# Gated linear attention feeding a GELU MLP: another row block releases W_in's first part, and two row transfers wait for a memset

## The chip, the cores and the metric

The kernel runs on one core of a Trainium2 chip. The metric is the device time of one execution in microseconds (us); lower is better. The engines are TensorE (PE; its weight loads are listed as PEld), VectorE (DVE), ScalarE (ACT), GpSimd (POOL) and SyncE (SP). SP and ACT issue transfers to a hardware queue of their own, POOL to a software queue. All three use the core's 16 DMA engines.

## The reference

Attention with a decaying state, in four batches of eight heads, 768 positions and 48 values a head; its output, as 3072 tokens of 384 values, goes through an MLP of width 2048.

```python
for t in range(S):
    state = alpha[:, :, t, :, None] * state + einsum('bhd,bhe->bhde', k[:, :, t], v[:, :, t])
    y[:, :, t] = einsum('bhd,bhde->bhe', q[:, :, t], state)
x = y.transpose(0, 2, 1, 3).reshape(B * S, H * D)
h = x @ w_in                                                     # 384 x 2048
g = 0.5 * h * (1 + tanh(sqrt(2 / pi) * (h + 0.044715 * h**3)))
out = g @ w_out                                                  # 2048 x 384
```

## The kernel before

**Tiling.** Positions are cut into six chunks of 128. A unit is one batch in one chunk; two units are a pair, and there are twelve pairs. For a pair, ACT takes the logarithm of alpha (`la`, L359), PE forms running sums over the 128 positions with a triangular matrix (`cum`, L346), and ACT takes exponentials of them with both signs (`b`, `binv`, L407). DVE scales q and k with these (`qp`, `kp`, L418). PE transposes the scaled rows (`qkT_ps`, L428) and multiplies them (`at`, L489), DVE masks the product (`atm`, L496), and PE makes `yps` from it and v (L546). It is narrowed (`x`), transposed (`xT`), and goes through the two MLP layers: `hT` (PE, L572, with W_in), GELU (ACT, L578), `acc` (PE, L591, with W_out). W_in lies in four tiles of 512 columns each, called parts 0 to 3 here; W_out in four as well.

**The order.** Every engine works through one list in order. For the first two pairs and some of the work behind them the order is written out by hand in `FIRST`: each step is an engine's letter and a task, as `P:cum0.0` (PE, first unit of pair 0) or `G:load.13` (POOL). The rest is placed by a planner with costs. The step `P:fill.7` puts seven products of a zero tile (`idle`, L289) on PE before the first `cum`.

**The loads.** Loads 0 to 11 are the row blocks of pairs 0 and 1, one unit of alpha, q or k each (192 KB). In order they are alpha of pair 0's two units (0, 1), q and k of its first unit (2, 3), q and k of its second (4, 5), alpha of pair 1's two units (6, 7), q and k of pair 1's first unit (8, 9), and q and k of its second (10, 11). SP issues all of them except 2 and 3, which ACT issues (`BY_ACT`). All other loads come from POOL, in the order of `LOADS`:

```python
LOADS = ('gatea 0 1', 'v0', 'gatek 0 1', 'in 0', 'v1', 'in 1', 'in 2', 'in 3', 'out 0', 'out 1', '2a', ...)
```

`v0` is v of pair 0, `in 0` is part 0 of W_in, `2a` the first unit's rows of pair 2. A `gate` step holds POOL: it is a copy of one column of a row block into a scratch tile (L314). It waits for that block's landing, and all of POOL's later issues stand behind it. `gatea 0 1` waits for load 1, and `gatek 0 1` for load 5 (k of pair 0's second unit). POOL has at most eight transfers outstanding. The ninth waits for the first to land, and so on.

PE reaches the first `hT` products in the order l10.0, l10.1, l10.3, l10.2, l10.5, l10.4, l10.6, l10.7 (`FIRST`); l10.n takes part n // 2 of W_in.

Of the kernel before, what the change touches and what calls it, by code (L numbers as in the profile page):

```python
# [7 lines left out]
F32 = mybir.dt.float32  # L8
# [163 lines left out]
class _Kernel:  # L172
# [3 lines left out]

    SPLIT = (2,)
    EARLY = (0, 1)
    LOADS = ('gatea 0 1', 'v0', 'gatek 0 1', 'in 0', 'v1', 'in 1', 'in 2', 'in 3', 'out 0', 'out 1', '2a', 'out 2', '2b', 'out 3', '3', '4', '5', '6', '7', '8', '9', '10', '11')

    PACKED, CUM_FF, R = (0, 1), (0, 1), 4
    RINGS = (('a', 0, 0, 1), ('a', 0, 1, 2), ('q', 0, 0, 1), ('k', 0, 0, 1), ('q', 0, 1, 2), ('k', 0, 1, 2),
# [436 lines left out]
    def tasks(self):  # L619
# [30 lines left out]
        for r, m, lo, hi in self.RINGS:  # L650
            loads[r, m, lo] = loads[r, m, hi - 1] = s.add(
                "load", {"ACT" if n in self.BY_ACT else "SP": W["ring_issue"]}, n, self.load(r, *pairs[m], lo, hi), land=(W["ring_v" if r == "v" else "ring"] * (hi - lo) // 2 if n else W["begin"]))
            n += 1
        for step in self.LOADS:
            if step[0] == "v":
# [209 lines left out]
    def run(self):  # L865
        nc, C = self.nc, self.C
        self.tasks()
        nc.vector.memset(self.zero, 0.0)
        nc.vector.memset(self.ones, 1.0)
        make_upper_triangular(nc, self.ut_h, val=1.0, diag=True)  # L870
        make_identity(nc, self.ident)
        nc.vector.memset(self.half, 0.0)
        for o in range(2):
            nc.vector.memset(self.half[64 * o:64 * o + 64, o:o + 1], 1.0)
        nc.vector.tensor_reduce(self.blk, self.ident.rearrange("p (g j) -> p j g", j=4), axis=mybir.AxisListType.X, op=ALU.max)
        same = self.blk[:, None, :].to_broadcast([C, C // 4, 4])
        nc.vector.tensor_tensor(self.ut_blk[1].rearrange("p (g j) -> p g j", j=4), self.ut_h.rearrange("p (g j) -> p g j", j=4), same, op=ALU.mult)
        nc.vector.tensor_tensor(self.ut_blk[0], self.ut_blk[1], self.ident, op=ALU.subtract)
        for i in range(max(self.BUFS[n] for n in self.ring)):
            for n in self.ring:  # L880
                if i < self.BUFS[n]:
                    nc.vector.memset(self.ring[n][i][:, :, :, self.D:64], 0.0)
        nc.vector.tensor_copy(self.ut, self.ut_h)
        order = self.s.order()
        for t in order:
            if t.load == LN_EXP:
                self.act_set(LN_EXP)
            t.emit(t.engine)
# [30 lines left out]
```

## Time and profile before

| | |
|---|---|
| median of 11 runs | 177.02 us |
| the runs, sorted | 176.65, 176.81, 176.89, 176.91, 176.93, 177.02, 177.61, 177.75, 177.83, 177.93, 178.12 |
| the profiled execution: its time | 178.63 us |
| the profiled execution: its span | 176.8 us |
| PE busy, of the span | 171.6 us (97%) |
| ACT busy | 128.8 us (73%) |
| DVE busy | 96.3 us (54%) |
| POOL busy | 57.7 us (33%) |
| moved by DMA | 28.86 MB, 163 GB/s |

The span runs from the first to the last instruction of the program; 1.83 us of the profiled execution lie outside of it. All times in the profile count from the start of the span. The chain of work that ended last is followed back from the last instruction, at each step to what released it. In the timeline a row merges like instructions that follow each other without a gap. A transfer's row gives its issue; its landing is a time from that issue on.

### The profile page before, as it was taken

To read this page: it belongs to the slowest core of one execution; us is meant where nothing else is said; L and a number is where in the kernel's file an instruction comes from. 1 tells how busy PE (TensorE), PEld (TensorE's weight loads), DVE (VectorE), ACT (ScalarE), POOL (GpSimd) and SP (SyncE) were. 2 spreads that over 40 slices of the span, in tenths; PEclk is the share of its full clock that TensorE was granted. 3 is DMA by queue.
4 is the path that set the end of the run, shared out by engine and by line. 5 is a ranking of instruction groups with operands and counts; after the bars stand their busy time and mean duration, and the time that the engine had idled before them with its cause. 6 is when DMAs were issued, how large, how long until landed. Compare 5 with 4: busy or idle time off the path is not lost.

```text
span 176.8 us, 4439 instructions
## 1 busy us (share of the span) xinstructions
PE 171.6 (97%) x1845; PEld 135.9 (77%) x1845; DVE 96.3 (54%) x191; ACT 128.8 (73%) x213; POOL 57.7 (33%) x64
## 2 busy tenths in 40 slices
PE   7899999999999999999999999999999999999993
PEld 2556899666886897797699689688697697796973
DVE  6289940066878996596499797494436415000000
ACT  2559799856977767858788967987988984481841
POOL 2596345996646766666530000000000000000000
PEclk9999999999999999999999999999999999999999
DMA  4999999999999999999999992262261360301102
GB/s 127 290 265 239 210 244 234 212 207 209 218 316 211 229 263 225 209 228 204 196 250 235 170 154 75 48 159 74 46 166 47 86 166 4 98 35 44 48 0 89
DMA packets 49621, 28.86 MB, mean 163 GB/s; under 512 B 37697, under 2 KB 46017, under 8 KB 49601
## 3 DMA queue, kind: packets, MB, share of 16 engines
q0 software_dynamic: 26464, 17.70, 60.3%
q1 hardware_dynamic: 22592, 10.49, 23.2%
q10 hardware_dynamic: 544, 0.39, 0.8%
q8 instruction: 14, 0.23, 0.6%
q14 instruction: 7, 0.05, 0.1%
HBM read 25.17 MB, written 4.72 MB: 169 GB/s over the span
## 4 chain that ended last, share of the span: by engine, by line
PE 93%; ACT 2%; DMA 2%; issue 0%
PE hT L572 36%; PE acc L591 35%; PE qkT_ps L428 4%; PE at L489 4%; PE yps L546 3%; DMA a<-in_alpha_dram 2%; PE yps L543 2%; PE kv L506 2%; PE cum L378 2%; PE cum L346 2%; PE idle L289 1%; PE xT_ps L560 1%; PE cum L380 1%; ACT qkT L446 1%; PE k_ps L454 1%; ACT la L359 1%
## 5 line engine op out<-in xcount | busy, mean ns | idle before, releaser
L572 PE MATMUL hT<-xT,w_in 128*128 128x256 bf16 x576 | 69.4, 273 | 0.0
L578 ACT ACTIVATE gT<-hT 128x512 bf16<-128x512 f32 x96 | 56.3, 600 | 17.7 <-PE hT L572 14.2
L591 PE MATMUL acc<-w_out,gT 128*128 128x384 bf16 (+3 forms) x416 | 69.0, 313 | 0.0
L572 PEld LDWEIGHTS <-w_in 128*128 128x128 bf16 x576 | 61.1, 113 | 1.6
L591 PEld LDWEIGHTS <-gT 128*128 128x128 bf16 x416 | 36.9, 97 | 19.2
L496 DVE TENSOR_TENSOR atm<-at,ut 128x512 bf16<-128x512 f32 x48 | 30.1, 682 | 12.7 <-PE at L489 12.6
L418 DVE TENSOR_TENSOR qp<-q,b 128x768 bf16<-128x768 f32 (+1 forms) x15 | 11.9, 795 | 14.9 <-ACT b L407 14.8
L418 DVE TENSOR_TENSOR kp<-k,binv 128x768 bf16<-128x768 f32 (+1 forms) x15 | 11.9, 792 | 10.6 <-ACT binv L407 10.6
L603 ACT COPY ot<-acc 128x384 f32<-128x384 f32 (+3 forms) x17 | 7.4, 439 | 13.0 <-PE acc L591 12.9
L308 POOL DMA_DIRECT2D q<-in_q_dram x11 | 12.2, 1105 | 7.5 <-DVE qp L418 1.8
L308 POOL DMA_DIRECT2D a<-in_alpha_dram x11 | 12.3, 1115 | 6.0 <-issue 2.2
L308 POOL DMA_DIRECT2D k<-in_k_dram x11 | 12.2, 1105 | 6.1 <-DVE st L531 2.4
L308 POOL DMA_DIRECT2D vb<-in_v_dram x11 | 12.1, 1101 | 4.8 <-DMA a<-in_alpha_dram 1.8
L407 ACT ACTIVATE b<-cum 128x768 bf16<-128x768 f32 (+1 forms) x15 | 10.3, 685 | 3.8 <-PE cum L380 2.3
L280 ACT ACT_TABLE_LOAD x9 | 11.5, 1283 | 0.9 <-PEq L903 0.7
L578 ACT ACT_TABLE_LOAD x9 | 11.5, 1283 | 0.2
L407 ACT ACTIVATE binv<-cum 128x768 bf16<-128x768 f32 (+1 forms) x15 | 10.2, 682 | 0.4 <-PE cum L350 0.4
L528 DVE TENSOR_TENSOR stmp<-kv,st 128x384 f32<-128x384 f32 x16 | 8.8, 553 | 2.0 <-PE kv L506 2.0
L446 ACT COPY qkT<-qkT_ps 128x512 bf16<-128x512 bf16 (+1 forms) x9 | 6.5, 728 | 4.2 <-PE qkT_ps L428 4.1
L553 DVE CAST x<-yps 128x384 bf16<-128x384 f32 x12 | 6.7, 556 | 5.0 <-PE yps L546 4.9
L531 DVE TENSOR_TENSOR st<-stmp,ends 128x384 bf16<-128x384 f32 x16 | 8.9, 558 | 0.6
L546 PE MATMUL yps<-vb,atm 128*128 128x48 bf16 x192 | 8.7, 183 | 0.1
(64 smaller groups left out, 158.1 us busy)
## 6 DMA issues: line engine op xcount, KB each, us to landing
out_dram<-ot SPq DMA_DIRECT2D x19, 192.0 KB, 5.2
a<-in_alpha_dram POOLq DMA_DIRECT2D x9, 384.0 KB, 11.9
q<-in_q_dram POOLq DMA_DIRECT2D x9, 384.0 KB, 11.5
k<-in_k_dram POOLq DMA_DIRECT2D x9, 384.0 KB, 11.4
vb<-in_v_dram POOLq DMA_DIRECT2D x9, 192.0 KB, 11.5
w_in<-in_moe_w_in_dram POOLq DMA_DIRECT2D x4, 384.0 KB, 8.9
w_out<-in_moe_w_out_dram POOLq DMA_DIRECT2D x4, 384.0 KB, 11.6
out_dram<-ot SPq DMA_DIRECT2D x9, 96.0 KB, 1.8
```

The costliest lines, as they stand in the source:

```text
L280: nc.scalar.add_instruction(mybir.InstLoadActFuncSet(name=nc.get_next_instruction_name(), act_func_set_id=i, engine=mybir.EngineType.Activ ...
L308: dma(u[t][:, lo:hi].rearrange("t b h d -> t (b h) d"), src.rearrange("b h s d -> s (b h) d")[c * C:(c + 1) * C])
L407: self.nc.scalar.activation(u[n].rearrange("t i h d -> t i (h d)")[:, lo:hi], cum, AF.Exp, scale=1.0 if n == "b" else -1.0)
L418: self.nc.vector.tensor_tensor(out, rows, b, op=ALU.mult)
L446: self.copy(e)(t, ps)
L496: self.nc.vector.tensor_tensor(u["atm", i][:, o], u["at", i][o], self.ut[:, None, :].to_broadcast([self.C, self.H // 2, self.C]), op=ALU.mult)
L528: nc.vector.tensor_tensor(s, acc, old, op=ALU.add)
L531: nc.vector.tensor_tensor(new.rearrange("f p (o d) -> f (p o) d", o=2), acc.rearrange("f p (o d) -> f (p o) d", o=2), ends, op=ALU.mult)
L546: nc.tensor.matmul(y[:, h, :], u["atm", i][:, h % 2, h // 2, :], u["vb"][:, i, h, :], start=c == 0, stop=True, skip_group_check=True)
L572: self.nc.tensor.matmul(h[:, s], w_in[:, j, nt % 4 + s], self.xT[c % self.NX][:, j, lo:hi].rearrange("p g t -> p (g t)"), start=j == 0, st ...
L578: return lambda e: self.nc.scalar.activation(self.gT[c % self.NG][:, nt:nt + 2, lo * self.C:hi * self.C], f.pop(("h", c, lo, nt)), AF.Gelu ...
L591: self.nc.tensor.matmul(f["acc", c, b][:, lo:hi], self.gT[c % self.NG][:, nt, b * self.C:(b + 1) * self.C], self.w_out[:, nt, lo:hi], star ...
```

## The change

Two edits. In `LOADS` the gate ahead of W_in's part 0 waits for another row block: `gatek 1 0` is load 9, k of pair 1's first unit. (The short title of the change speaks of q; the code names k, and the built program's copy into the gate tile reads k.) Its place in POOL's order stays. And in `run` the tile that loads 2 and 4 fill, q of pair 0, is made early, and DVE writes zeros into one column of its first unit. Load 2 writes the same place, so that ACT's issue of it now waits for this memset; load 3 stands behind it in ACT's queue. In DVE's list the memset stands third, after those of `zero` and `ones`. No other instruction moves on any engine.

```diff
-    LOADS = ('gatea 0 1', 'v0', 'gatek 0 1', 'in 0', 'v1', 'in 1', 'in 2', 'in 3', 'out 0', 'out 1', '2a', ...)
+    LOADS = ('gatea 0 1', 'v0', 'gatek 1 0', 'in 0', 'v1', 'in 1', 'in 2', 'in 3', 'out 0', 'out 1', '2a', ...)
...
         nc.vector.memset(self.zero, 0.0)
         nc.vector.memset(self.ones, 1.0)
         make_upper_triangular(nc, self.ut_h, val=1.0, diag=True)
+        first = self.p[0, 0]["q"] = self.tile("q", [C, 2, self.H, self.D], F32)
+        nc.vector.memset(first[:, 0, 0, 0:1], 0.0)
         make_identity(nc, self.ident)
```

More of the change, by code (lines that the diff above doesn't have):

```diff
@@ L178 @@
     EARLY = (0, 1)
-    LOADS = ('gatea 0 1', 'v0', 'gatek 0 1', 'in 0', 'v1', 'in 1', 'in 2', 'in 3', 'out 0', 'out 1', '2a', 'out 2', '2b', 'out 3', '3', '4', '5', '6', '7', '8', '9', '10', '11')
+    LOADS = ('gatea 0 1', 'v0', 'gatek 1 0', 'in 0', 'v1', 'in 1', 'in 2', 'in 3', 'out 0', 'out 1', '2a', 'out 2', '2b', 'out 3', '3', '4', '5', '6', '7', '8', '9', '10', '11')
     PACKED, CUM_FF, R = (0, 1), (0, 1), 4
```

## The prediction

> **What bounds the kernel now.** The page comes first. PE is busy for 97% of the span, and the chain that ended last is PE's for 93%. So in most of the kernel whatever moves PE moves the end by the same time. The chain in order of time then shows the stretch in which that isn't so yet.
>
> ```profile
> PE 171.6 (97%) x1845; PEld 135.9 (77%) x1845; DVE 96.3 (54%) x191; ACT 128.8 (73%) x213; POOL 57.7 (33%) x64
> PE 93%; ACT 2%; DMA 2%; issue 0%
> 0.74 3.91 DMA a<-in_alpha_dram
> 4.67 0.53 ACT la L359
> 5.25 1.44 PE cum L346 x7
> ```
>
> The head hangs on one transfer: alpha of pair 0's first unit, issued at 0.74, landed at 4.65. ACT's logarithm follows, then the running sums. From there on the chain runs through engines, PE mostly, and no other load is on it. From 18.4 on it is nearly all PE. So two things can matter: when the first alpha block lands, and whether a POOL load becomes late for PE. The timelines of POOL and PE give the second.
>
> ```profile
> 7.68 0.25 POOL L314 COPY gate<-k 128x1 f32<-128x1 f32 x1 [0.61 <-DMA k<-in_k_dram]
> 8.15 0.74 POOL L321 DMA_DIRECT2D w_in<-in_moe_w_in_dram  x1 [0.21 <-issue]
> 8.88 1.18 POOL L308 DMA_DIRECT2D v<-in_v_dram  x1
> 10.06 2.25 POOL L321 DMA_DIRECT2D w_in<-in_moe_w_in_dram  x3
> 21.84 1.47 PE L572 MATMUL hT<-xT,w_in 128*128 128x256 bf16 x12
> 23.35 0.83 PE L572 MATMUL hT<-xT,w_in 128*128 128x256 bf16 x6
> 24.35 0.82 PE L572 MATMUL hT<-xT,w_in 128*128 128x256 bf16 x6
> ```
>
> Asked one by one, W_in's four parts land 7.0, 8.3, 9.4 and 10.6 us after their issues at 8.15, 10.06, 10.79 and 11.56: at 15.2, 18.4, 20.2 and 22.2. PE first takes them at 18.39, 21.01, 22.49 and 24.35. Each is 2.2 to 3.2 us early. Part 3 has the least room, 2.2 us, at l10.6.
>
> **The hold on ACT's transfers.** It adds one DVE memset of 128x1 (60 ns by its neighbour `ones`). It delays `half` and what follows by that much, but `blk` waits for POOL's `ident` until 1.81 anyway, so this costs nothing. ACT's two issues started at 0.77 and 1.50. They now start at about 1.2, when the third memset is done, and 1.95: 0.45 us later. Who pays: q and k of the first unit landed at 4.5 and 5.1 and are taken at 7.33 and 7.81, so nobody does. Who gains is read from the queues between 2.0 and 4.2 us, where q10 is ACT's and q1 SP's:
>
> ```profile
> q10 hardware_dynamic: 384, 0.28, 51.0%
> q1 hardware_dynamic: 271, 0.20, 28.6%
> ```
>
> ACT's queue moved more than SP's, although the first alpha block (0.20 MB) was all that the head waited for. With ACT's start 0.45 us later and its mean rate of 0.15 MB/us (0.28 MB in 1.9 us) kept, and with the 335 GB/s that the window from 3 to 4 us shows for both, alpha's block is through at T, where 0.20 + 0.15 x (T - 2.7) = 0.48 - 0.335 x (4.2 - T). So T is 3.87, and it lands 0.33 us earlier. The ends: 0, if the slow start of SP's queue (5 packets up to 2.7 us) is its own; 0.85, if ACT's data stayed wholly behind it. I take 0.33. The second alpha block gains less, but its logarithm has 0.5 us to spare before `cum` on PE. The chain after it is made of engines' own times, and the loads it uses (k of pair 0 at 7.6, v0 at 11.8 for 13.56) are early enough. So PE would reach W_in 0.33 us sooner, unless W_in is late.
>
> **The moved gate.** It waits for load 9 instead of load 5. Load 5 landed at 3.10 + 4.4 = 7.55, and W_in's part 0 was issued 0.60 later. Load 9 was issued at 5.74, so it landed at 10.1; part 0 is issued at 10.7, 2.55 us later. Behind the gate stand all of POOL's loads: v1, W_in's other parts, W_out, and rows from pair 2 on. SP and ACT pass no gate. What the delay is worth depends on what the DMA engines do meanwhile, told by POOL's queue q0 in three windows (8.7 to 9.0, 11.2 to 11.5, 11.5 to 12.0):
>
> ```profile
> q0 software_dynamic: 4, 0.02, 13.6%
> ...
> q0 software_dynamic: 2, 0.00, 0.6%
> ...
> q0 software_dynamic: 48, 0.05, 61.2%
> ```
>
> v0, issued at 5.79, moved its first packets at 8.7. W_in's part 0, issued at 8.15, moved its own at 11.5, after a lull: 3.0 and 3.35 us from issue to first packet. So with an issue at 10.7 the stream starts at about 14.05. SP's rows are through by about 12 then, and the engines idle for two microseconds. The stream took 10.66 us from 11.5 to part 3's landing at 22.16. Of that, 0.42 us went to SP's last rows (0.08 + 0.05 MB between 11.5 and 14 at about 300 GB/s); these are out of the way now. So 10.24 us are left: part 3 lands at 24.3, part 2 at 22.4.
>
> Here a rule speaks against my number. The Trainium skill, DMA: Bandwidth & Descriptors, "Latency and other measured facts", gives about 1 us to a software queue's first byte. By that the stream would start at 11.7, right behind SP's rows, slip by no more than 0.4 us and cost nothing. The rows say 3.0 and 3.35; I take the rows.
>
> **The sum, in the profiled execution.** PE is ready for part 2 at 22.49 - 0.33 = 22.16 and waits 0.22 (22.38), then for part 3 at 24.24 and waits 0.06. Head -0.33, waits +0.28: the net is -0.05, and 178.63 becomes 178.6. Later loads shift by 2.1 and still hold: the tightest are alpha of pair 2's second unit (lands 32.7, taken 34.92), W_out's part 2 (32.0, 34.6) and alpha of pair 3 (38.2, 40.54), with 2.2 to 2.6 us of room. If the slip grew by 0.3, ACT would wait for the first of them at little cost to PE, which has `acc` products there.
>
> **From there to the median.** The profiled execution is slower than all eleven runs. These fall into two groups: six from 176.65 to 177.02 (mean 176.87) and five from 177.61 to 178.12 (mean 177.85), 0.98 apart. The rows suggest why: the groups by shape give the `idle` products of 512 columns 567 ns each in the window from 0 to 10 us and 379 from 9.7 to 20:
>
> ```profile
> L289 PE MATMUL idle<-zero 128*128 128x512 bf16 x12 | 5.2, 567 | 1.2 <-DVE half L872 1.2
> ...
> L289 PE MATMUL idle<-zero 128*128 128x512 bf16 x7 | 2.3, 379 | 0.0
> ```
>
> The profile's clock column says 1.00 in both, so the row decides: PE's early products are slow. The Trainium skill, TensorE: Matmul & The Clock Gate, "What's actually happening", says that full rate comes after a busy window of about 3.4 us, and that the windows run freely, so that the moment differs between executions. One trace can't show that. Without the rule all runs would share my profile's slack, and the median would go to 176.97. With it the profiled execution, late to warm up, stands for the slow group, and in the fast group PE reaches W_in 0.98 us sooner: room 1.2 us instead of 2.2. With the gate moved, such an execution wants part 3 at 24.35 - 0.98 - 0.33 = 23.04, gets it at 24.3, and loses 1.26: net +0.93, to 177.80. The slow group gives 177.85 - 0.05 = 177.80. Both end at the time that W_in's landing allows, 177.8. The split of the times into two groups persuades me, not strongly.
>
> **Rivals.**
> - *It cancels out* (chance 0.33). The groups have another cause than PE's early rate, or the slip is 1.7 us rather than 2.1. Then the head's gain and W_in's waits cancel: 176.7 to 177.4, about 177.0. For it: the sum in the one trace that there is. Against it: the two groups.
> - *Faster* (0.17). The first packet comes sooner than 3 us after the issue when the software queue has drained. The mechanism is the start of POOL's queue at W_in's part 0; its price is the slip. It decides where the slip stays under about 0.9 us, the fast group's room (1.2) less the head's 0.33. Then nothing waits and the head's 0.33 counts; also PE's idle time before `cum` (0.89 us) is shorter, which could help it to full rate earlier. 176.5.
> - *Later loads too* (0.05). A slip of 2.6 makes part 3 wait 0.5 more, and alpha of pairs 2 and 3 come late: 178.3.
> - *The gate waits for q, as the title has it.* The built program's gate copy reads k. Load 8 would be only 0.6 us earlier (5.08 + 4.4); the forecast would be 177.2.
>
> **How the numbers follow.** The forecast, W_in late for PE in most executions, has 0.45 and 177.8, with 177.5 to 178.1 as its own range. From 176.6 to 178.2 the range takes in the canceled case and part of the faster one. Within 0.3% (about what a measurement of this kernel can tell from no change) is 176.49 to 177.55. Slower: 0.05 and nearly all of 0.45, so 0.48; same 0.35; faster 0.17.
>
> **What would show it.** In the changed profile the first `la` should start at 4.2 to 4.5 instead of 4.67, the gate's copy near 10.2, W_in's first issue near 10.7, its first packets near 14 and part 3's landing near 24.3, with PE idle before l10.5 or l10.6. If q0 moves W_in's data before 13 us, or PE shows no gap between 20 and 25 us, the forecast is wrong. If the runs still fall into groups a microsecond apart, my account of them is.

## The result, and the profile after

The changed kernel takes 179.8 us (median of 12 runs, 178.65 to 180.86), the kernel before 177.61 beside it (47 runs). The ratio of their times is 1.0123, 95% interval 1.0093 to 1.0153: slower by 1.2%, where 0.4% was forecast. The twelve runs spread evenly over 2.2 us. (Medians are of all runs of a kernel; ratios leave out runs more than 1.5% above its fastest.) The profiled execution took 179.23 us, with a span of 177.5. First the page after, its busy times and the chain by engine:

```profile
PE 170.3 (96%) x1845; PEld 135.0 (76%) x1845; DVE 96.9 (55%) x192; ACT 128.9 (73%) x213; POOL 57.8 (33%) x64
PE 84%; DMA 10%; SPq 3%; POOL 2%; issue 1%; ACT 0%; POOLq 0%
```

PE's share of the chain fell from 93 to 84% and DMA's rose from 2 to 10%. The chain in order of time (start, length, what) names the transfers on it:

```profile
13.46 8.72 DMA w_in<-in_moe_w_in_dram
...
99.02 3.87 DMA xT<-x
```

Behind the block that the gate waits for (5.51 to 10.21) there are two, some 80 us apart: W_in, which PE takes near 22, as forecast, and the transpose of x that fills `xT`, which PE takes near 103 and which the forecast did not have. The timelines of ACT, POOL and PE after, in this order, answer to the rows of before:

```profile
3.76 0.52 ACT L359 ACTIVATE la<-a 128x384 f16<-128x384 f32 x1 [1.74 <-DMA a<-in_alpha_dram]
```

```profile
10.34 0.18 POOL L314 COPY gate<-k 128x1 f32<-128x1 f32 x1 [3.92 <-DMA k<-in_k_dram]
10.80 0.75 POOL L321 DMA_DIRECT2D w_in<-in_moe_w_in_dram  x1 [0.29 <-issue]
```

```profile
20.32 0.85 PE L572 MATMUL hT<-xT,w_in 128*128 128x256 bf16 x6 [0.25 <-DMA w_in<-in_moe_w_in_dram]
...
22.22 0.85 PE L572 MATMUL hT<-xT,w_in 128*128 128x256 bf16 x6 [0.23 <-DMA w_in<-in_moe_w_in_dram]
...
24.14 1.07 PE L572 MATMUL hT<-xT,w_in 128*128 128x256 bf16 x8
```

The logarithm starts 0.91 us earlier than before, part 0 is issued at 10.80, and W_in's parts land at 16.61, 20.27, 22.17 and 24.09. So l10.6 starts 0.05 us after part 3's landing, at 24.14; in the profile of before it started at 24.35. Up to there the kernel gained 0.2 us in this pair of traces. Then comes the place that was overlooked. PE before, PE after:

```profile
102.28 0.82 PE L572 MATMUL hT<-xT,w_in 128*128 128x256 bf16 x6
```

```profile
102.93 0.82 PE L572 MATMUL hT<-xT,w_in 128*128 128x256 bf16 x6 [0.67 <-DMA xT<-x]
```

SP issues those transposes, in its own queue. SP's timeline of before, then of after:

```profile
94.59 1.29 SPq L472 DMA_TRANSPOSE xT<-x  x1
96.56 1.23 SPq L466 DMA_TRANSPOSE qkT<-qp  x1
97.88 1.21 SPq L472 DMA_TRANSPOSE xT<-x  x1
```

```profile
94.41 1.29 SPq L472 DMA_TRANSPOSE xT<-x  x1
96.37 2.56 SPq L466 DMA_TRANSPOSE qkT<-qp  x1
99.02 1.21 SPq L472 DMA_TRANSPOSE xT<-x  x1
```

The first one is issued within 0.2 us of the same time in both, but it lands at 99.02 before and at 101.63 after. The second, the one that PE waits for, lands at 100.26 and 102.89: SP issues it 1.1 us later, because issuing the transpose between them took 2.56 us instead of 1.23, and it then takes 1.5 us longer. The last rows that POOL loads land at 98.64 and 101.44. In all 18 profiles of this study the first of these transposes lands 0.1 to 0.5 us after POOL's last rows. The DMA queues between 94 and 102 us (packets, MB, share of the 16 engines; q0 is POOL's, q1 SP's), before and after, show what they share:

```profile
q1 hardware_dynamic: 3052, 0.88, 56.0%
q0 software_dynamic: 833, 0.71, 44.4%
```

```profile
q0 software_dynamic: 2088, 1.12, 89.9%
q1 hardware_dynamic: 1582, 0.40, 51.0%
```

POOL moves 0.41 MB more in that stretch, and SP's queue gets through half as much.

### The profile page after: what moved, and what is told of

It is laid out like the page before. It is cut to its first block, busy times and chain, and to the rows that moved or that the text cites. A ratio compares the mean times of both kernels' runs of the same rounds, so it can differ in the third digit from the quotient of the medians.

```text
span 177.5 us, 4440 instructions
## 1 busy us (share of the span) xinstructions
PE 170.3 (96%) x1845; PEld 135.0 (76%) x1845; DVE 96.9 (55%) x192; ACT 128.9 (73%) x213; POOL 57.8 (33%) x64
## 4 chain that ended last, share of the span: by engine, by line
PE 84%; DMA 10%; SPq 3%; POOL 2%; issue 1%; ACT 0%; POOLq 0%
PE hT L572 35%; PE acc L591 34%; DMA w_in<-in_moe_w_in_dram 5%; PE at L489 3%; PE qkT_ps L428 3%; DMA k<-in_k_dram 3%; SPq L305 3%; PE yps L546 2%; DMA xT<-x 2%; PE yps L543 2%; PE kv L506 2%; PE cum L378 2%; PE xT_ps L560 1%; POOL w_in L321 1%; POOL v L308 1%; PE cum L380 1%
## 5 line engine op out<-in xcount | busy, mean ns | idle before, releaser
L308 POOL DMA_DIRECT2D k<-in_k_dram x11 | 12.2, 1107 | 7.1 <-DMA vb<-in_v_dram 2.0
L308 POOL DMA_DIRECT2D q<-in_q_dram x11 | 12.2, 1110 | 6.1 <-DVE ot L603 1.8
L407 ACT ACTIVATE b<-cum 128x768 bf16<-128x768 f32 (+1 forms) x15 | 10.2, 683 | 3.2 <-PE cum L380 2.3
L407 ACT ACTIVATE binv<-cum 128x768 bf16<-128x768 f32 (+1 forms) x15 | 10.2, 680 | 0.2 <-PE cum L350 0.2
## 6 DMA issues: line engine op xcount, KB each, us to landing
a<-in_alpha_dram POOLq DMA_DIRECT2D x9, 384.0 KB, 12.2
```

Of the source, the lines that this page charges most:

```text
L308: dma(u[t][:, lo:hi].rearrange("t b h d -> t (b h) d"), src.rearrange("b h s d -> s (b h) d")[c * C:(c + 1) * C])
L407: self.nc.scalar.activation(u[n].rearrange("t i h d -> t i (h d)")[:, lo:hi], cum, AF.Exp, scale=1.0 if n == "b" else -1.0)
```

## The experiments

Two theories stood against the one of the forecast (the gate makes W_in late): that the hold costs, and that PE's moment of full rate does. "l10.6" is the start of its first product, "last rows" the landing of POOL's last transfer, "xT wait" PE's wait near 102 us, all from the one profile of each kernel; ratios are to the kernel before, run beside.

| kernel | ratio [95%] | l10.6 | last rows | xT wait |
|---|---|---|---|---|
| before | 1 | 24.35 | 98.64 | 0 |
| after | 1.0123 [1.0093, 1.0153] | 24.14 | 101.44 | 0.67 |
| gate_only | 1.0126 [1.0073, 1.0179] | 23.44 | 100.19 | 0.27 |
| hold_only | 1.0003 [0.9976, 1.0030] | 22.82 | 99.10 | 0 |
| after_cut | 1.0122 [1.0069, 1.0175] | 24.11 | 98.81 | 0 |
| before_cut | 0.9976 [0.9953, 0.9999] | 22.54 | 98.37 | 0 |
| after_w0 | 1.0123 [1.0074, 1.0173] | 23.30 | 104.78 | 3.74 |
| before_w0 | 1.0061 [1.0038, 1.0085] | 24.34 | 98.33 | 0 |
| v1_first | 1.0050 [1.0025, 1.0076] | 25.07 | 98.59 | 0 |
| early | 1.0009 [0.9985, 1.0034] | 23.42 | 99.23 | 0 |
| after_both | 1.0094 [1.0060, 1.0128] | 22.45 | 101.44 | 2.21 |
| before_both | 0.9966 [0.9944, 0.9988] | 22.45 | 96.67 | 0 |
| gate_q | 1.0051 [1.0022, 1.0081] | 24.07 | 100.68 | 0 |
| hold_early | 1.0015 [0.9992, 1.0038] | 22.84 | 99.70 | 0.41 |
| after_cut9 | 1.0020 [0.9983, 1.0057] | 23.35 | 99.76 | 0 |
| before_cut9 | 0.9967 [0.9943, 0.9991] | 22.45 | 95.69 | 0 |
| fill8 | 1.0013 [0.9994, 1.0031] | 23.78 | 99.28 | 0 |
| after_look | one run, 178.58 us | 24.04 | 100.62 | 0 |

**Which half of the change costs.** gate_only moves the gate without the hold, hold_only the other way round.

```diff
# gate_only: the first line alone; hold_only: the two memset lines alone
-    LOADS = (... 'v0', 'gatek 0 1', 'in 0', ...)
+    LOADS = (... 'v0', 'gatek 1 0', 'in 0', ...)
...
+        first = self.p[0, 0]["q"] = self.tile("q", [C, 2, self.H, self.D], F32)
+        nc.vector.memset(first[:, 0, 0, 0:1], 0.0)
```

> The moved gate alone, without the memset that holds ScalarE's transfers. Theory A (the gate lets POOL's whole stream of loads start two microseconds later, and the stream never makes them good): nearly all of the loss is here, ratio to before 1.010 to 1.016; POOL's last row block lands near 101 instead of 98.6, W_in's part 3 near 24. Theory B (the hold makes k of the first unit late, 7.3 instead of 5.1, and that costs): ratio 1.000 to 1.003. Theory C (the difference is TensorE's warm-up falling otherwise): about half of the loss, 1.005.

> The memset that holds ScalarE's transfers alone, with the gate where it was. Theory A: 0.996 to 1.001, a little faster, since alpha's first block lands near 3.7 and W_in is in time. Theory B: 1.008 to 1.012, with PE waiting for the first kp. Theory C: 1.005.

gate_only took 179.27 us, hold_only 177.39, before beside them 177.06. The whole loss is the gate's, so neither of the two theories fits it. PE's waits in the profile of gate_only (us in total, times, longest) are at the same two places:

```profile
PE hT L572 <- DMA w_in<-in_moe_w_in_dram: 0.6, 2, 0.4
PE hT L572 <- DMA xT<-x: 0.3, 1, 0.3
```

**The late loads relieved alone.** after_cut and before_cut load only half of W_out's parts 2 and 3 and use the loaded half twice, so the output is not the reference's. POOL's stream is 393 KB, or 1.9 us, shorter behind W_in; PE's products are the same in number and shape. (In this cut and those below, a line with `...` is shortened.)

```diff
+                m = w if part < 2 else w // 2
-    self.w_out[:, part * w:(part + 1) * w, :], ...[part])
+    self.w_out[:, part * w:part * w + m, :], ...[part][:, 0:m])
...
-    self.w_out[:, nt, lo:hi]
+    self.w_out[:, nt if nt < 8 else nt // 4 * 4 + nt % 2, lo:hi]
```

> Both edits, and of W_out's parts 2 and 3 only half is loaded (the second half of each part is not loaded; its products take the loaded half), the products as many as before. That takes as many bytes out of POOL's stream as one part of W_in, 1.9 us of it, after W_in. Theory A in full (the stream's end is what is paid for, near 100 us): the loss goes, ratio to before 0.996 to 1.004. If instead PE's wait for W_in near 22 us is what is paid for, it stays at 1.010 to 1.014. Theories B and C: it stays.

> The kernel before with the same half of W_out's parts 2 and 3 not loaded (products as many as before, on the loaded half). Theory A: if POOL's stream already binds the kernel before in some executions, 0.990 to 0.997 and less spread; if it has room there, 1.000. Theories B and C: 1.000.

The last rows came at 98.81 and nothing waited near 102, yet the pair is still 1.0122 over 0.9976, or 1.46% apart. The profile of after_cut, its fastest run, shows the other place, a wait of 0.7 us, and l10.6 at 24.11 against 22.54, which is the 1.6 us between the two spans:

```profile
PE hT L573 <- DMA w_in<-in_moe_w_in_dram: 0.7, 1, 0.7
```

**W_in relieved alone.** In after_w0 and before_w0 the first layer of chunk 0 takes part 0 for all products (not the reference's output again), so no product there waits for parts 1 to 3. Loads are unchanged.

```diff
-            w_in = self.w_in[nt // 4].rearrange(...)
+            w_in = self.w_in[nt // 4 if c else 0].rearrange(...)
```

> Both edits, but the first layer of chunk 0 (the products that wait for W_in near 20 to 24 us) takes part 0 in place of all four parts; parts 1 to 3 are still loaded, and chunks 1 to 5 take them as before. Theory D (PE's wait for W_in's parts near 22 us is nearly all of the loss): ratio to before 0.998 to 1.003, the first layer's long run starts at 22.5 to 23.5. Theory A (what the late stream costs near 100 us is most of it): 1.006 to 1.012, with a wait for xT near 102 us.

> The kernel before with chunk 0's first layer on part 0 alone, as the control. Theory D with W_in in time in the kernel before: 1.000. If W_in binds some executions of the kernel before too: 0.994 to 0.998.

Against the kernel before the loss did not go: 1.0123. Against its own control it is 1.0123 over 1.0061, 0.6% (about 0.1 to 1.2, the two intervals combined), so this pair leaves open how much went. The profile of after_w0 is of its longest run (184.03 us; the other five took 178.79 to 183.32), so only its kind of wait is read here:

```profile
106.15 0.82 PE L572 MATMUL hT<-xT,w_in 128*128 128x256 bf16 x6 [3.74 <-DMA xT<-x]
```

Parts 1 to 3 no longer hold PE (l10.6 at 23.30 instead of 24.14), and the wait stands at the transpose. before_w0 became slower than before, which no theory had and no run here explains: 16 of its 22 runs lie above 178.3 us, and its profile has PE at full rate only from 9.24 us. Being late to full rate was rarer in the kernel before (39 of its 209 runs beside these kernels lie above 178.3).

**Less delay of the gate.** v1_first moves v1 ahead of the gate, so that less stands behind it; early lets the gate wait for load 3 in the kernel before.

```diff
# v1_first (and G:load.13 ahead of G:gate.1 in FIRST)
+    LOADS = (... 'v0', 'v1', 'gatek 1 0', 'in 0', 'in 1', ...)
# early
+    LOADS = (... 'v0', 'gatek 0 0', 'in 0', 'v1', ...)
```

> The moved gate without the hold, but v of the second pair goes ahead of the gate, so that the DMA engines have 384 KB more to move while POOL waits (1.4 us of the two that they idle). Theory A and D, both by way of the idle engines: W_in's part 3 lands 1.2 to 1.5 us sooner than with the gate alone, and most of the loss goes, 1.001 to 1.006. If the loss comes from the order of W_in against SP's rows and not from idle DMA engines: it stays at 1.010 to 1.013.

> The other way: W_in's gate waits for k of the first pair's first unit (lands at 5 to 7 us), two places earlier than in the kernel before, no hold. Theory A: the stream ends up to 0.8 us sooner, and W_in with it; 0.994 to 0.999, with fewer executions in the upper tail of the times. If SP's row blocks that it then shares the engines with are what PE needs next: 1.002 to 1.006.

v1_first took 178.52 us and early 177.85, before beside them 177.37. The ratio of v1_first, 1.0050, is as expected, but its profile shows another loss than W_in's: part 3 landed at 22.86, PE waited for no part, and l10.6 still started only at 25.07. PE had full rate from 4.33, then idled ahead of the second `cum`, for alpha's second block, and its clock record has half rate again from 7.74 to 11.15:

```profile
7.09 0.85 PE L346 MATMUL cum<-la,ut_blk 128*128 128x384 f16 x7 [1.31 <-ACT la L359]
```

So PE's rate in the head can cost what W_in costs, and what v1_first recovers of W_in is not separated from it. early says less than it was meant to: in its profile the first gate, on alpha's second block (landed at 6.32), held v0's issue until 6.49, and W_in's part 0 was issued at 8.29, no sooner than before (8.15).

**Both places relieved.** after_both and before_both join the two edits above.

> Both edits, with both cures at once: chunk 0's first layer takes part 0 of W_in alone (parts 1 to 3 are still loaded), and only half of W_out's parts 2 and 3 is loaded (their products take the loaded half). Theory E (two places pay, each able to hide the other: W_in near 22 us and the late stream near 102 us; with one cured the other takes the loss): against its control, before_both, 0.997 to 1.003, and no wait of PE for W_in's parts 1 to 3 or for xT. If something else in the late start costs, for instance v of the second pair or W_out, it stays 1.005 to 1.012 above the control.

> The control: the kernel before with the same two cures (part 0 alone in chunk 0's first layer; half of W_out's parts 2 and 3 not loaded). 0.995 to 1.006 of before, depending on how often PE reaches full rate at 6 and how often at 9.4 us.

after_both (179.17 us) is still 1.28% above before_both (176.9). Its W_in wait is gone and its l10.6 is that of the control; the cut of 1.9 us had not been enough for the other place. PE's rows near 102 of after_both, then of before_both:

```profile
102.88 0.81 PE L573 MATMUL hT<-xT,w_in 128*128 128x256 bf16 x6 [2.21 <-DMA xT<-x]
```

```profile
100.38 0.82 PE L573 MATMUL hT<-xT,w_in 128*128 128x256 bf16 x6
```

The difference near 102 is 2.5 us, all of the loss in this pair of traces. The queues between 94 and 102 us, of before_both and of after_both, show why:

```profile
q1 hardware_dynamic: 4118, 1.18, 71.6%
q0 software_dynamic: 83, 0.26, 11.0%
```

```profile
q0 software_dynamic: 1717, 0.96, 79.8%
q1 hardware_dynamic: 1627, 0.40, 57.8%
```

In the control POOL has 0.26 MB left in that stretch. In after_both it has 0.96, and the transposes share the engines with it: POOL's k rows, three times in a row, land 2.3 (at 88.58), 3.35 (96.14) and at the end 4.8 us (101.44) later than the control's. The transposes are issued from 92.8 on, so the slip grows once they start.

**Dose and hold.** gate_q waits for load 8 (q of pair 1's first unit, as the short title of the change has it) without the hold; hold_early has the hold and the gate on load 3.

```diff
# gate_q
+    LOADS = (... 'v0', 'gateq 1 0', 'in 0', ...)
# hold_early: the two memset lines, and
+    LOADS = (... 'v0', 'gatek 0 0', 'in 0', ...)
```

> The gate as the change's title has it: W_in waits for q of the second pair's first unit, which stands one place ahead of k in SP's queue (9.5 against 10.1 us in the profile of before). No hold. Theory E with a threshold (the stream has about a microsecond of room, the rest is paid in full): 1.005 to 1.010, between the kernel before and gate_only, W_in's part 3 near 23.5. If it is the same as gate_only, 1.012, the landing of the block is not what sets the start of the stream.

> The hold together with an earlier gate (k of the first pair's first unit). If the hold's worth is an earlier full rate of PE (clock record at 6 instead of 9.4 us in nearly all executions), and what it lacks is W_in in time: 0.994 to 0.998, with l10.6 starting near 22.5. If k of the first unit, which the hold makes late, gates it: 1.000 to 1.004, since W_in then leaves later too (k lands near 7.1 with the hold).

gate_q (178.3 us, before 177.17) shows the W_in place by itself. Its profile has no wait for `xT`:

```profile
20.24 0.85 PE L572 MATMUL hT<-xT,w_in 128*128 128x256 bf16 x6 [0.59 <-DMA w_in<-in_moe_w_in_dram]
...
22.16 0.85 PE L572 MATMUL hT<-xT,w_in 128*128 128x256 bf16 x6 [0.25 <-DMA w_in<-in_moe_w_in_dram]
```

It costs 0.5%, near what was forecast for the whole change. By the load that it waits for, the gate costs 0.5% (load 8) and 1.3% (load 9) against load 5. hold_early waited 0.41 us for `xT` with an early gate and stayed at 1.0015, within its uncertainty of the kernel before; the gain hoped for did not come.

**Both places relieved by more.** after_cut9 and before_cut9 keep the W_in edit and load only a quarter of W_out's parts 1 to 3: 885 KB, 4.3 us of the stream. Again the output is not the reference's.

```diff
+                m = w if part < 1 else w // 4
...
+    self.w_out[:, nt if nt < 4 else nt // 4 * 4, lo:hi]
```

> As after_both (chunk 0's first layer on part 0 of W_in alone), but of each of W_out's parts 1 to 3 only a quarter is loaded (the other three quarters are not loaded; the products, as many as before, take the loaded one): 885 KB less in the stream, 4.3 us instead of 1.9. Theory F (after_both still paid because the stream was still late for xT, whose transposes then share the engines with POOL's last rows): PE's wait for xT goes, last rows land by 99, ratio to its control 0.998 to 1.003. If a later start of W_in costs by another way than W_in's and xT's lateness: still 1.008 to 1.013 above the control.

> The control for after_cut9: the kernel before with the same two changes (part 0 alone in chunk 0's first layer; a quarter of W_out's parts 1 to 3 loaded). 0.994 to 0.998 of before.

Here more than half of the loss went: 177.58 us against 177.02, and 1.0020 over 0.9967 = 1.0053 (about 1.001 to 1.010, the two intervals combined). That lies between the two expectations, so the two places hold most of the loss and not demonstrably all. PE of after_cut9 near 102:

```profile
101.42 0.81 PE L573 MATMUL hT<-xT,w_in 128*128 128x256 bf16 x6
```

There is no wait for `xT`. The 0.9 us left in this pair of traces stand already at l10.6 (23.35 against 22.45). Part 0, which this edit doesn't relieve, landed at 16.90 and was taken at 16.94, where the control takes it at 16.49: 0.45 of the 0.9 is W_in again. The gate's block had landed late in that run, at 11.37.

**A busier PE in the head.** fill8 gives PE an eighth `idle` product ahead of the first `cum` (`P:fill.8`), to make full rate come early in every execution. after_look is the changed kernel once more.

> The kernel before with eight idle products ahead of the first cum instead of seven, 0.43 us more of PE work in the gap before cum. If PE's full rate comes at 6 rather than 9.4 us where that gap is short, and executions with the late one make the upper group of the times: the upper group gets smaller, 0.996 to 0.999. If the groups have another cause: 1.000 to 1.002.

> The changed kernel once more, one look. Theory E and F: what differs between its executions is when the gate's block lands (9.4 to 11.6 us) and how long PE waits for xT near 102 (0.3 to 3.7 us); W_in's part 3 lands between 23.4 and 25.5 here, and the span is 152.3 us plus the start of l10.6 plus the wait for xT.

fill8 had no run above 178.04 us in 22, while 8 of 51 runs of before beside it lay above 178.3: the rare long ones were not seen, but the ratio did not fall (1.0013). Its runs still form two groups, 15 up to 177.29 and 7 from 177.55. after_look shows W_in waits of 0.20 and 0.41 us and none for `xT`, with its last rows at 100.62. So the second place varies between executions of one kernel.

## Why the forecast was right in sign and short in size

**Head: right sign, too small.** The first alpha block landed at 3.74 instead of 4.65, a gain of 0.91 and not 0.33, just beyond the upper end of 0.85. (The forecast's own equation gives T = 3.90, a gain of 0.30.) The hold as a whole brought nothing all the same, as hold_only's 1.0003 shows. "Nobody does" pay for the hold was not right in this trace: k of the first unit landed at 7.27 instead of near 5.5, and PE waited for what is made of it:

```profile
7.98 0.40 PE L428 MATMUL qkT_ps<-ident,kp 128*128 128x128 bf16 x4 [0.64 <-DVE kp L418]
```

**Gate and W_in: right.** The copy came at 10.34 (forecast 10.2), the issue at 10.80 (10.7), part 3 at 24.09 (24.3). PE waits 0.25 for part 1, which the forecast had in time, 0.23 for part 2 (0.22), and takes part 3 0.05 after its landing. gate_q shows that this place alone can cost about what the whole was forecast at. The start of the stream was subtler than its sign: q0 between 12.2 and 13 us of after:

```profile
q0 software_dynamic: 32, 0.03, 70.3%
```

First packets moved at 12.38, 1.6 us after the issue, so ahead of the 13 us that I had set as a sign against me. But 0.03 MB up to 13 us is little (0.15 followed in the next microsecond), and the landing came out as worked. (In the trace of before the first packets of v0 and of part 0 move 3.1 and 3.4 us after their issues.) Neither the rule's 1 us nor my 3 is the whole of it: by the first packet the rule is nearer, by the landing the rows are.

**The step that failed: "Later loads shift by 2.1 and still hold".** I went through POOL's later loads by what takes them, and each did have room. I left out what SP moves meanwhile. The transposes of x near 94 us are no POOL load and pass no gate, but they land with POOL's last rows, 2.6 us later than before, and PE takes them at 102. The shift did not stay at 2.1 either: POOL's last rows came 2.8 us later. The Trainium skill, DMA: Bandwidth & Descriptors, "Issuing engines are not separate DMA queues", says that all issue paths feed the same 16 engines; the windows from 94 to 102 show it. Against the transposes' landing, PE's start at 102.28 had 2.0 us of room in the profile of before, which was late to full rate. An execution that is earlier has less. hold_only took that transpose, landed at 100.72, at once, at 100.77:

```profile
100.77 0.82 PE L572 MATMUL hT<-xT,w_in 128*128 128x256 bf16 x6
```

"Still hold" would have been read from an execution with much room, even with the transposes in the list.

**The term mis-sized: 0.98 us for early full rate.** PE's rate in its first microseconds does differ between executions. The rows by shape from 4 to 9 us, before and after:

```profile
L346 PE MATMUL cum<-la,ut_blk 128*128 128x288 f16 x4 | 1.8, 444 | 0.0
```

```profile
L346 PE MATMUL cum<-la,ut_blk 128*128 128x288 f16 x4 | 1.1, 284 | 0.0
```

Where PE idles 0.89 to 0.97 us ahead of the first `cum`, full rate comes from 9.2 to 9.4 us (before, before_w0) and l10.6 at 24.35. Where it idles 0.57 or less, it comes by 4.1 to 6.7 in every trace with a clock record (two have none), and in three of these nothing else delays l10.6, which starts at 22.45 to 22.54 (before_cut, before_both, before_cut9). That is 1.8 to 1.9 us earlier. So such an execution has less room at W_in than the 1.2 worked out: before_cut takes part 3 0.2 us after its landing, hold_only at once (22.77, 22.82). W_in's floor near 24.1 takes 1.6 to 1.7 from them, where a net 0.93 was forecast. The two groups of the first eleven runs, 0.98 apart, were not the measure of it: the profiled execution, late to full rate, took 178.63 us and lies outside both, as most runs of before_w0 do. What splits these groups looks like another thing, not tested: early and fill8 were profiled at 177.69 and 178.01 us, with full rate by 5.9 and 6.7, but alpha's second block landed at 6.32 and 6.53 instead of 4.8 to 5.05, and l10.6 started at 23.42 and 23.78.

**The sum.** One line fits all 18 profiles within 0.4 us: the span is 152.4 us, and l10.6's start, and the xT wait (after_w0 with 0.7 more for W_out and 1.7 for its clock). after: 152.4 + 24.14 + 0.67 = 177.2 (177.5). before_both: 152.4 + 22.45 = 174.85 (174.9). (In after_w0 the 0.7 is a wait in its trace, the 1.7 half of its 3.41 us at half rate.) So W_in and `xT` are the two places, and a cure of the one leaves PE to wait at the other. From an early execution to the trace of after they make 1.6 to 1.7 and 0.67 us, together 2.3, near the 2.2 between the medians, though that trace's time lies 0.6 below its median. How the 1.2% is split is not shown: gate_q, with W_in's place alone, lost 0.5%, after_cut, with the late rows relieved, lost all.

**What stays open.** The two profiles of after (spans 177.5 and 176.8) lie in the lower half of its runs, so no trace shows what the longest (180.86) wait for. Where the gate waits for load 9, that block lands anywhere from 9.4 to 11.6 in these profiles and W_in's part 3 from 22.9 to 25.6, and the xT wait varies from 0 to 3.7; both would do. A fall back to half rate, as in v1_first, would do as well. No version tried is faster than the kernel before with its whole output kept.

## What to carry to other kernels

When a stream of loads is shifted, look for every transfer that shares the DMA engines with its tail, on other engines' queues too, and not only for the users of the shifted loads. Read the room at each place for the earliest execution, not for the one profiled. Where relieving one wait leaves the time as it was, relieve the next wait as well before you acquit the first.

## What the runs showed of the hardware

- Transposes on SP's queue that shared the engines with POOL's rows landed when those ended, in all 18 profiles: the first of them 4.4 us after its issue before, 7.2 after, 8.8 in after_both.
- After the wait of 3.74 us in after_w0, PE's clock record has half rate for one window of 3.41 us, from 107.45 to 110.86; the page's clock row shows the dip:

```profile
PEclk9999999999999999999999978999999999999999
```

- With 0.89 and 0.97 us of idle time ahead of the first `cum` full rate came at 9.35 and 9.24 us, with 0.57 or less by 6.7. After 1.31 us ahead of the second `cum` (v1_first) the rate fell back for one such window, 7.74 to 11.15.
- ACT's and SP's first blocks do not land evenly: k of the first unit came anywhere from 4.9 to 7.3 us in kernels without the hold, the first alpha block from 3.8 to 4.7.
